# Zero rows of seven experts cut to 128 each, row ids masked by count, and one load freed of another expert's zero rows

## The chip, the cores and the metric

The kernel runs on one core of a Trainium2 chip. The metric is the device time of one execution in microseconds (us), taken as the median of several runs. The engines are PE (matrix products), PEld (its weight loads), DVE and ACT (vector and scalar work), POOL (GpSimd) and SP (which issues most DMAs). A read "chain" below is a row of steps in which each waits for the one before.

## The reference

Attention with a window of 128 positions and a distance bias runs over 8 batches, 8 heads and 576 positions; its output is 4608 rows (tokens) of 512 values. A layer of eight experts follows, in which each token goes to one expert:

```
logits = xn @ en.T / tau
expert_idx = np.argmax(logits, axis=1)
...
for e in range(E):
    mask = expert_idx == e
    h = np.maximum(x[mask] @ w1[e], 0.0)
    out[mask] = gate_w[mask, None] * (h @ w2[e])
```

w1 is 512 x 1024 and w2 is 1024 x 512 for each expert. How many tokens an expert gets is known only at run time.

## The kernel before

**Two stages.** The attention stage ends near 250 us of the trace. For each tile of 128 tokens it writes the rows with a scattering DMA from POOL (line 884) into a table in device memory, `xs`. In it each expert has a segment; a row is 521 words: 512 for the token's values (as two halves in fp16, high and low), one for the token's id, eight for its logits. The attention stage also does the first 512 rows of one expert, the "head" (`PARTS`, `HEAD`), as soon as those rows are there. The stage of the experts, `moe`, follows.

**Ranks and slots.** The experts are ranked by their counts. Rank 0 is the head's expert; what is left of it are rows 512 to 671. `SLOTS` gives each rank a fixed number of rows (672, 688, 624, 576, 544, 528, 528, 512), and `TURNS` the order of work: ranks 0, 1, 4, 3, 5, 6, 2, 7. Rows over whole blocks of 128 ("tails" of 32 or 64 rows) of several ranks share one pass through PE (`PACKED`).

**Zero rows.** A slot is larger than its expert's count, so rows past the count hold nothing. `blank(s)` (line 1318) reads the count from `n0i` or `nki` into a register of SP and writes rows from a constant `zrow` behind the last token: 704, 544, 576, 544, 544, 640 and 512 rows for ranks 1, 4, 3, 5, 6, 2 and 7, and 160 for rank 0. Each zero row has the id PAD, 2^20, which the last scatter into the output skips.

**Loads.** `rows(s)` (line 1329) then loads the slot twice: as `info` (rows on partitions, lines 1336 and 1349) and turned by the DMA as `xT` (line 1345). Rank 0 loads `info` alone (lines 1336, 1342, 1349), and PE turns it (line 1372). Both DMAs have addresses known only at run time, so the framework makes a load wait for every earlier write into `xs` that isn't declared free.

**Ids.** `row_info(s)` (line 1383) puts the ids of the slot's rows into a tile of their own: for rank 0 DVE masks those past the count `n0` with PAD (lines 1401 and 1402); for the others POOL copies them (line 1404). `put` scatters each block of 128 output rows by these ids (line 437).

**Weights and products.** The weights come in 512 KB pieces `ws` (lines 1435 and 1437, six buffers); ACT makes the high half of each (line 1455), DVE the low half (line 1453). `hidden` (line 1478) fills one of eight PSUM buffers for each of eight column groups, in one or two chunks of rows; ACT and DVE take them out as `hh` and `hl` (lines 1488 and 1486); `output` (line 1522) multiplies by w2, and DVE or ACT scale the result to `y` (lines 1536 and 1534).

**Order.** A planner written in the kernel (`Plan`) places every step as a job with an engine, an assumed length and a due time, and emits them in that order; on each engine the order is then fixed, and an engine that waits holds up all that is queued behind it. On SP, `blank` of rank 0, `blank` of rank 1 and one piece of weights stand ahead of `rows` of rank 0. After the experts' stage stands code for rows that don't fit the slots (lines 1675 to 1786); its DVE operations are placed among those of the last experts.

Of the kernel before, what the change touches and what calls it, by code (L numbers as in the profile page):

```python
# [15 lines left out]
F32 = mybir.dt.float32  # L16
I32 = mybir.dt.int32
AF = mybir.ActivationFunctionType
ALU = mybir.AluOpType
# [4 lines left out]
P = 128  # L24
# [3 lines left out]
PAD = 1 << 20  # L28
# [13 lines left out]
HEAD = PARTS[-1][1]  # L42
# [121 lines left out]
def kernel(  # L164
# [11 lines left out]
    nc = tc.nc  # L176
    NTOK, DM = out.shape
# [12 lines left out]
    def sync_dep(after, before):  # L190
        tc.add_manual_dep(
            after.ins,
            before.ins.name,
            mybir.DependencyInfo(mybir.DependencyClass.Sync, mybir.DependencyReason.DATA),
            reason="rows written by scattering DMAs",
        )
# [119 lines left out]
    def kt_(nm, shape, dt=F32):  # L316
        if nm not in sel_:
            sel_[nm] = keep.tile(shape, dt, name=nm)
        return sel_[nm]
# [37 lines left out]
    def count_ops(z):  # L357
        V = nc.vector

        def ke(nm):  # L360
            return kt_(nm, [P, E])

        return [
            ("DVE", 90, lambda: V.tensor_copy(ke("cnt"), z["cnt"])),
            ("DVE", 90, lambda: V.tensor_tensor(ke("hn"), ke("ho"), ke("cnt"), op=ALU.mult)),
            ("DVE", 90, lambda: V.tensor_reduce(kt_("n0", [P, 1]), ke("hn"), axis=AX.X, op=ALU.add)),
            ("DVE", 90, lambda: V.tensor_copy(kt_("n0i", [P, 1], I32), kt_("n0", [P, 1]))),
        ]

    def rank_ops(z):  # L370
# [919 lines left out]
    def moe(mctx):  # L1290
# [18 lines left out]
        def choose(s):  # L1309
# [5 lines left out]
            if s == 0:  # L1315
                state[s].update(w1=(w["w1h"], w["w1l"]), w2=(w["w2h"], w["w2l"]))

        def blank(s):
            e, (nb, hb), b0 = state[s]["e"], blocks(s), first_row(s) // P
            n = nc.sync.value_load(sel_["n0i"][0:1, 0:1] if s == 0 else sel_["nki"][0:1, s : s + 1], min_val=0, max_val=NTOK)  # L1320
            m = (nb - b0) * P + hb
            d = nc.sync.dma_start(
                xs[ds(e, 1), ds(n, m), :].rearrange("o (a p) c -> p (o a) c", p=32),
                zrow[0:32].unsqueeze(1).to_broadcast([32, m // 32, ROW]),
            )
            for p_ in scatters + loads:
                tc.declare_no_dep(d.ins, p_.ins, reason="rows beyond the expert's tokens, not read yet")

        def rows(s):
            cap, r0, (nb, hb) = SLOTS[s], first_row(s), blocks(s)  # L1330
            b0 = r0 // P
            e = state[s]["e"]
            xx = xt.tile([P, 2 * KT, MAXCAP], F16, tag="xT", name=f"xT_{s}")
            info = yp.tile([P, MB, ROW], F32, tag="info", name=f"info_{s}", bufs=INFOS)
            dl = [
                nc.sync.dma_start(
                    info[:, b0:nb, :],
                    xs[ds(e, 1), r0 : nb * P, :].rearrange("o (a p) c -> p (o a) c", p=P),
                )
            ]  # L1340
            if s == 0:
                dl.append(nc.sync.dma_start(info[:hb, nb, 0:DM], xs[ds(e, 1), nb * P : nb * P + hb, 0:DM].rearrange("o p c -> (o p) c")))
            else:
                x_ = xs[ds(e, 1), r0:cap, 0:DM].rearrange("o s c -> (o s) c").bitcast(F16)
                dl.insert(0, nc.sync.dma_start(xx[:, :, r0:cap], x_, transpose=True))
            if hb:
                nc.gpsimd.memset(info[:, nb, DM + 1 : ROW], 0.0)
                dl.append(
                    nc.sync.dma_start(
                        info[tail_rows(s), nb, :],  # L1350
                        xs[ds(e, 1), nb * P : nb * P + hb, :].rearrange("o p c -> (o p) c"),
                    )
                )
            loads.extend(dl)
            for d in dl:
                for p_ in scatters:
                    sync_dep(d, p_)
            state[s].update(xT=xx, info=info)

        turned = {}  # L1360
# [22 lines left out]
        def row_info(s):  # L1383
            (nb, hb), b0, info = blocks(s), first_row(s) // P, state[s]["info"]
            ids = yp.tile([P, MB], I32, tag="ids", name=f"ids_{s}", bufs=2)
            gs = yp.tile([P, MB], F32, tag="gs", name=f"gs_{s}", bufs=2)
            jobs = [(slice(0, P), slice(b0, nb), ids[:, b0:nb])]
            if hb:
                pr, pk = tail_rows(s), packs.setdefault(PACKED[s][0], {})
                if not pk:  # L1390
                    pk["ids"] = yp.tile([P, 1], I32, tag="ids2", name=f"ids2_{s}", bufs=2)
                    pk["gs"] = yp.tile([P, 1], F32, tag="gs2", name=f"gs2_{s}", bufs=2)
                jobs.append((pr, slice(nb, nb + 1), pk["ids"][pr]))
            past = yp.tile([P, MB], I32, tag="past", name=f"past_{s}", bufs=2)
            place = yp.tile([P, MB], F32, tag="place", name=f"place_{s}", bufs=1) if s == 0 else None
            for pr, bl, i_ in jobs:
                if s == 0:
                    nc.gpsimd.iota(
                        place[pr, bl], pattern=[[P, bl.stop - bl.start]], base=bl.start * P, channel_multiplier=1, allow_small_or_imprecise_dtypes=True
                    )  # L1400
                    nc.vector.tensor_scalar(past[pr, bl], place[pr, bl], sel_["n0"][pr], float(PAD), op0=ALU.is_ge, op1=ALU.mult)
                    nc.vector.tensor_tensor(i_, info[pr, bl, DM].bitcast(I32), past[pr, bl], op=ALU.max)
                else:
                    nc.gpsimd.tensor_copy(i_, info[pr, bl, DM].bitcast(I32))  # L1404
            n = nb + (hb > 0)
            n2 = yp.tile([P, MB], F32, tag="n2", name=f"n2_{s}", bufs=2)
            if hb:
                nc.gpsimd.memset(n2[:, nb : nb + 1], 1.0)  # L1408
            t = yp.tile([P, MB * (3 + E)], F32, tag="gt", name=f"gt_{s}", bufs=2)
            state[s].update(ids=ids, gs=gs, n2=n2, gate=gate_ops(n2[:, b0:n], info[:, b0:n, DM + 1 : ROW], gs[:, b0:n], t, yp.tile([P, MB], F32, tag="ry", name=f"ry_{s}", bufs=2)))  # L1410

        def span(s, a):
            return tail_rows(s) if a == blocks(s)[0] else slice(0, P)
# [124 lines left out]
        def put(s, a):  # L1538
            put_rows(packs[s]["ids"] if a == "t" else state[s]["ids"][:, a : a + 1], ys[s, a])
# [8 lines left out]
        def before(name):  # L1548
            return [(name, ORDER)]
# [15 lines left out]
        for p, s in enumerate(TURNS):  # L1565
# [12 lines left out]
                f"info{s}", "POOL", 900, lambda s=s: row_info(s), after=[f"rows{s}"], makes=[("rows", ("rows", s))],  # L1578
                uses=[("info", s)], due=t0 - 6000,
            )  # L1580
            prev = []
            for a in range(b0, nb + (hb > 0)):
                J(f"sum{s}_{a}", "POOL", 1120, lambda a=(s, a): info_sum(*a), after=[f"info{s}"], makes=[("xsum", ("xsum", s, a))], uses=[("info", s)], due=t0 - 5000)
# [56 lines left out]
            for a in todo + list(range(b0, nb)):  # L1640
                n = f"{s}_{a}"
                n_out += 1
                two = (s, a) == last_out
                key = ("y", n)
                for i in range(1 + two):
                    c = slice(i * DM // 2, (i + 1) * DM // 2) if two else slice(0, DM)
                    if a == "t":
                        mem = [m for m in PACKED if PACKED[m][0] == s]
                        PEJ(
                            f"out{n}_{i}", 24 * (216 + 22 * (len(mem) - 1)), lambda s=s: output_pack(s),  # L1650
                            [f"tail{m}" for m in mem] + w2,
                            makes=[("pt", ("ps2", n, i))], uses=[("w", 2, m) for m in mem] + [("h", s)], due=t0,
                        )
                    else:
                        PEJ(
                            f"out{n}_{i}", 24 * 216 / (1 + two), lambda x=(s, a, c): output(*x), halves + w2,
                            makes=[("pt", ("ps2", n, i))], uses=[("w", 2, s), ("h", s)], due=t0,
                        )
                    e = ("ACT", "DVE")[(n_out + i) % 2]
                    J(  # L1660
                        f"y{n}_{i}", e, 658 / (1 + two), lambda x=(s, a, e, c): scaled(*x), after=[f"out{n}_{i}"] + [f"gated{m}" for m in (mem if a == "t" else [s])],
                        makes=[] if i else [("y", key)], uses=[("ps2", n, i), key, ("rows", s)], due=t0,
                    )
                J(
                    f"put{n}", "POOL", 1150, lambda x=(s, a): put(*x), after=[f"y{n}_{i}" for i in range(1 + two)], uses=[key, ("rows", s)],
                    due=t0, dma=750,
                )
        plan.run(handed["free"])
# [155 lines left out]
```

## Time and profile before

| what | us |
|---|---|
| median of 3 runs (633.00 to 635.02) | 634.11 |
| the profiled execution | 637.05 |
| its span in the trace | 635.00 |
| PE busy | 581.0 (91%) |
| DVE, ACT, POOL busy | 360.8, 337.2, 302.0 |

The profiled execution took 2.05 us more than its span and 2.94 us more than the median. Times of the trace count from the span's start. A busy PE is not PE at its peak: how fast it runs depends on its granted clock too, of which 1.00 is 2.4 GHz and 0.50 is 1.2 GHz.

### The profile page before, as it was taken

The page shows a single profiled execution, that of the slowest core. Times are in us where ns is not written, and L with a number is a line of the kernel's source. Part 1 is how long each engine was busy: PE and PEld are TensorE (multiplying, and loading weights), DVE is VectorE, ACT ScalarE, POOL GpSimd, SP SyncE. Part 2 cuts the span into 40 slices and gives each one's busy share as a digit, 9 for nine tenths or more (in the row PEclk, how much of TensorE's full clock was granted, in tenths as well). Part 3 has the DMA queues.
Part 4 walks back from the last instruction along what each step waited for, and adds up shares of the span by engine and source line. Part 5 has one row for each costly group of instructions (what it writes and reads, how often), then busy time and mean ns, then how long its engine had stood idle before and what let it go on. Part 6 is the DMA issues. An engine that isn't in the chain of part 4 may idle for free. (4 is left out here: it accounts for less than half of the span.)

```text
span 635.0 us, 16631 instructions
## 1 busy us (share of the span) xinstructions
PE 581.0 (91%) x6273; PEld 381.7 (60%) x6273; DVE 360.8 (57%) x1381; ACT 337.2 (53%) x786; POOL 302.0 (48%) x447
## 2 busy tenths in 40 slices
PE   6899999798868999699699999899999999999993
PEld 3677677566647767276435855655856845744442
DVE  6889999889858746167191361445451454831220
ACT  4899999799758943057271550453541634410310
POOL 7689899999848896212322310234311311511111
PEclk9989999999969999989989999999999999999998
DMA  7689998999797465899999249919693077001000
GB/s 239 182 202 247 247 225 222 264 275 248 195 312 177 103 160 180 216 264 362 244 290 270 92 117 255 338 61 305 208 257 141 1 198 245 35 33 47 0 34 34
DMA packets 119954, 119.44 MB, mean 188 GB/s; under 512 B 79125, under 2 KB 80149, under 8 KB 119872
## 3 DMA queue, kind: packets, MB, share of 16 engines
q1 hardware_dynamic: 114032, 99.32, 60.5%
q0 software_dynamic: 5840, 19.05, 8.2%
q8 instruction: 50, 0.82, 0.5%
q14 instruction: 32, 0.26, 0.1%
HBM read 71.82 MB, written 28.11 MB: 157 GB/s over the span
## 5 line engine op out<-in xcount | busy, mean ns | idle before, releaser
L1478 PE MATMUL ps<-xT,w1h 128*128 128x272 f16 (+8 forms) x896 | 170.0, 291 | 3.0 <-DVE y L1536 1.9
L1478 PE MATMUL ps<-xT,w1l 128*128 128x272 f16 (+8 forms) x448 | 129.9, 291 | 0.0
L1478 PEld LDWEIGHTS <-w1h 128*128 128x128 f16 x896 | 87.6, 99 | 31.9 <-issue 3.4
L641 ACT ACTIVATE pe<-sb,nm 128x128 f32<-128x128 f32 x288 | 94.8, 393 | 16.8 <-DVE nm L633 15.3
L1522 PE MATMUL ps<-w2h,hh 128*128 128x512 f16 (+1 forms) x256 | 96.1, 375 | 6.1 <-DVE hl L1486 6.1
L437 POOL DMA_INDIRECT out_dram<-y,ids x31 | 35.8, 1155 | 137.3 <-DVE y L1536 68.4
L1522 PE MATMUL ps<-w2l,hh 128*128 128x512 f16 (+1 forms) x256 | 95.9, 375 | 0.0
L1522 PE MATMUL ps<-w2h,hl 128*128 128x512 f16 (+1 forms) x256 | 95.8, 374 | 0.0
L1486 DVE SCALAR_TENSOR_TENSOR hl<-ps,hh 128x272 f16<-128x272 f32 (+8 forms) x112 | 49.9, 463 | 70.8 <-ACT hh L1488 70.3
L1522 PEld LDWEIGHTS <-hh 128*128 128x128 f16 x512 | 50.1, 98 | 63.5 <-issue 7.9
L1488 ACT ACTIVATE hh<-ps 128x272 f16<-128x272 f32 (+8 forms) x112 | 43.7, 413 | 56.0 <-PE ps L1478 55.3
L555 ACT ACTIVATE pq<-ptp 128x512 f16<-128x512 f32 x87 | 63.9, 743 | 11.4 <-PE ptp L650 6.9
L1453 DVE SCALAR_TENSOR_TENSOR w2l<-ws,w2h 128x1024 f16<-128x1024 f32 x28 | 34.1, 1228 | 56.1 <-ACT w2h L1455 56.0
L606 PE MATMUL sc<-k,q 64*64 64x192 f32 (+1 forms) x1152 | 62.3, 333 | 0.0
L650 PE MATMUL ptp<-ident,pe 128*128 128x128 f32 x288 | 54.9, 296 | 5.7 <-ACT pe L641 4.4
L428 POOL TENSOR_TENSOR xsum<-info 128x512 f32<-128x512 f16 (+2 forms) x37 | 42.8, 1178 | 34.5 <-ACT junk L431 30.3
L1455 ACT ACTIVATE w2h<-ws 128x1024 f16<-128x1024 f32 x28 | 29.1, 1052 | 52.5 <-DMA ws<-moe_w_dram 52.5
L633 DVE CUSTOM_DVE_ANT_0 sb<-sc,tab_full 128x128 f32<-128x128 f32 x224 | 55.3, 280 | 0.2
L1478 PEld LDWEIGHTS <-w1l 128*128 128x128 f16 x448 | 44.1, 99 | 14.0 <-issue 0.4
L558 DVE SCALAR_TENSOR_TENSOR pq<-ptp,pq 128x512 f16<-128x512 f32 x57 | 42.4, 744 | 8.8 <-ACT pq L555 8.0
L650 PEld LDWEIGHTS ptp<-ident,pe 128*128 128x128 f32 x288 | 33.8, 144 | 19.1 <-ACT pe L641 12.4
L1534 ACT ACTIVATE y<-ps,gs 128x512 f32<-128x512 f32 (+1 forms) x16 | 10.7, 671 | 64.4 <-PE ps L1522 59.8
(256 smaller groups left out, 1189.6 us busy)
## 6 DMA issues: line engine op xcount, KB each, us to landing
ws<-moe_w_dram SPq DMA_DIRECT2D x56, 512.0 KB, 6.7
q<-q_dram SPq DMA_DIRECT2D x36, 256.0 KB, 4.8
ldv<-v_dram SPq DMA_DIRECT2D x36, 256.0 KB, 4.7
k<-k_dram SPq DMA_DIRECT2D x32, 256.0 KB, 4.6
info<-xs SPq DMA_DIRECT2D x5, 1042.0 KB, 6.3
stg<-moe_w_dram SPq DMA_DIRECT2D x16, 256.0 KB, 5.5
xs<-zrow SPq DMA_DIRECT2D x3, 1107.1 KB, 7.8
info<-xs SPq DMA_DIRECT2D x2, 1302.5 KB, 10.4
```

Source lines behind the costliest of these rows:

```text
L428: nc.gpsimd.tensor_tensor(o_, x[:, 0:DM], x[:, DM : 2 * DM], op=ALU.add)
L437: ins = nc.gpsimd.indirect_dma_start(out[:, :], bass.IndirectOffsetOnAxis(ap=ids, axis=0), y, None, bounds_check=NTOK - 1, oob_is_err=False)
L555: nc.scalar.activation(hi, ps, AF.Copy, scale=scale)
L558: nc.vector.scalar_tensor_tensor(lo, ps, scale, hi, op0=ALU.mult, op1=ALU.subtract)
L606: nc.tensor.matmul(sc[T, hf, j][l * REM : (l + 1) * REM, i, c0 : c0 + (n1 - n0) * REM].rearrange("p (n c) -> p n c", c=REM), qT[T][rows, h ...
L633: nc.vector.tensor_tensor_reduce(sb_t[T, hf][:, 2 * j + i, :], sc[T, hf, j][:, i, c0 : c0 + P], tab, -QS, BIG, ALU.add, ALU.min, nm_t[T, h ...
L641: nc.scalar.activation(pr_t[T, hf][:, n, :], sb_t[T, hf][:, n, :], AF.Exp, bias=nm_t[T, hf][:, n : n + 1], scale=-1.0)
L650: nc.tensor.matmul(pt.rearrange("p (l j) c -> p l j c", j=2)[:, :, j, i * REM : (i + 1) * REM], pe[:, n, :], ident.rearrange("p (l c) -> p ...
L1478: nc.tensor.matmul(ps[:, :w], a[:, kt, fs], xx[:, b + kt, c0 : c0 + w], start=(n == 0), stop=(n == len(jobs) - 1))
L1486: nc.vector.scalar_tensor_tensor(hl[:, ft, c0 : c0 + w], ps[:, :w], 0.0, hi, op0=ALU.max, op1=ALU.subtract)
L1488: nc.scalar.activation(hi, ps[:, :w], AF.Relu)
L1522: nc.tensor.matmul(ps, x[:, ft, a * P : (a + 1) * P], w[:, ft, c], start=(n == 0), stop=(n == len(jobs) - 1))
```

## The change

- `count_ops`: the integer count of rank 0, `n0i`, is at least HEAD (512).
- `blank`: for every rank but 0 the zero rows are 128 from the count on, and no longer the whole slot's length. Rank 0 keeps 160.
- `rows`: the loads of a rank are declared free of the zero rows of other ranks.
- `row_info` and the new `row_ids`: POOL no longer copies ids. For every rank POOL writes a table of places (`iota`), and DVE masks the ids by the rank's count. This is a job of its own, placed behind the sixth `hl` of the rank's first chunk; `put` waits for it.

```
-            ("DVE", 90, lambda: V.tensor_copy(kt_("n0i", [P, 1], I32), kt_("n0", [P, 1]))),
+            ("DVE", 90, lambda: V.tensor_scalar(kt_("n0i", [P, 1], I32), kt_("n0", [P, 1]), float(HEAD), None, op0=ALU.max)),
...
+        zeros = []
...
         def blank(s):
...
-            m = (nb - b0) * P + hb
+            m = (nb - b0) * P + hb if s == 0 else P
...
+            zeros.append((s, d))
...
             for d in dl:
                 for p_ in scatters:
                     sync_dep(d, p_)
+                for s_, p_ in zeros:
+                    if s_ != s:
+                        tc.declare_no_dep(d.ins, p_.ins, reason="rows of another expert")
...
-            place = yp.tile([P, MB], F32, tag="place", name=f"place_{s}", bufs=1) if s == 0 else None
+            place = yp.tile([P, MB], F32, tag="place", name=f"place_{s}", bufs=2)
             for pr, bl, i_ in jobs:
-                if s == 0:
-                    nc.gpsimd.iota(
...
-                    nc.vector.tensor_scalar(past[pr, bl], place[pr, bl], sel_["n0"][pr], float(PAD), op0=ALU.is_ge, op1=ALU.mult)
-                    nc.vector.tensor_tensor(i_, info[pr, bl, DM].bitcast(I32), past[pr, bl], op=ALU.max)
-                else:
-                    nc.gpsimd.tensor_copy(i_, info[pr, bl, DM].bitcast(I32))
+                nc.gpsimd.iota(
...
+            state[s]["known"] = jobs, past, place
...
+        def row_ids(s):
+            jobs, past, place = state[s]["known"]
+            n = sel_["n0"] if s == 0 else sel_["nk"][:, s : s + 1]
+            for pr, bl, i_ in jobs:
+                nc.vector.tensor_scalar(past[pr, bl], place[pr, bl], n[pr], float(PAD), op0=ALU.is_ge, op1=ALU.mult)
+                nc.vector.tensor_tensor(i_, state[s]["info"][pr, bl, DM].bitcast(I32), past[pr, bl], op=ALU.max)
...
+            J(
+                f"ids{s}", "DVE", 400, lambda s=s: row_ids(s), after=[f"info{s}"] + before(f"hlo{s}_{chunks(s)[0][0]}_5"),
+                uses=[("info", s), ("rows", s)], due=t0,
+            )
...
-                    f"put{n}", "POOL", 1150, lambda x=(s, a): put(*x), after=[f"y{n}_{i}" for i in range(1 + two)], uses=[key, ("rows", s)],
+                    f"put{n}", "POOL", 1150, lambda x=(s, a): put(*x), after=[f"y{n}_{i}" for i in range(1 + two)] + [f"ids{m}" for m in (mem if a == "t" else [s])], uses=[key, ("rows", s)],
```

The order of instructions on PE, ACT and SP is the same before and after. What differs on SP are the waits. SP at the end of the attention stage, before; `xs<-zrow` is the zero rows (of rank 1 here), `ws` weights, `info` the rows of rank 0, and in brackets stand the counters that a DMA waits for (HW: DMAs of SP, eight in turn; SW: DMAs of POOL, the scatters). The zero rows of rank 0 count on HW2, those of rank 1 on HW3:

```order
L1322 DMA xs<-zrow 32x22x521 [waits DMAHW2_49]
L1435 ISA
L1435 DMA ws_1_0_6444<-moe_w_dram 128x1024
L1336 ISA
L1336 DMA info_6447<-xs 128x521 [waits DMASW4_49,DMASW3_49,DMASW5_49,DMASW2_49,DMAHW0_49,DMASW1_49,DMAHW1_49,DMASW0_49,DMAHW3_49,DVE_49,DMAHW7_49,PE_49,Activation_49]
```

The same place after:

```order
L1324 DMA xs<-zrow 32x4x521 [waits DMAHW2_49]
L1444 ISA
L1444 DMA ws_1_0_6444<-moe_w_dram 128x1024
L1339 ISA
L1339 DMA info_6447<-xs 128x521 [waits DMASW3_49,DMASW4_49,DMASW2_49,DMASW5_49,DMASW1_49,DMAHW0_49,DMASW0_49,DMAHW1_49,DVE_49,DMAHW7_49,PE_49,Activation_49]
```

The wait for HW3 is gone from the load of rank 0; it stands now at the first load of rank 1.

DVE where the hidden products of rank 2 begin, before; `w2l` is the last piece of weights of rank 7, `hl` empties a PSUM buffer, and `nk`, `eb` begin the operations for rows that don't fit:

```order
L1453 SCALAR_TENSOR_TENSOR w2l_9323<-ws_7_3_9330,w2h_9322 128x1024
L1486 SCALAR_TENSOR_TENSOR hl_9381<-ps_2_0_0_9367,hh_9380 128x320
L1486 SCALAR_TENSOR_TENSOR hl_9381<-ps_2_0_1_9389,hh_9380 128x320
L1486 SCALAR_TENSOR_TENSOR hl_9381<-ps_2_0_2_9411,hh_9380 128x320
L1486 SCALAR_TENSOR_TENSOR hl_9381<-ps_2_0_3_9426,hh_9380 128x320
L1486 SCALAR_TENSOR_TENSOR hl_9381<-ps_2_0_4_9441,hh_9380 128x320
L1486 SCALAR_TENSOR_TENSOR hl_9381<-ps_2_0_5_9456,hh_9380 128x320
L1683 COPY nk_10121<-nk 128x8
L1684 COPY eb_10122<-eb 128x8
```

And after:

```order
L1696 COPY nk_10152<-nk 128x8
L1697 COPY eb_10153<-eb 128x8
L1698 COPY eb_10153<-eb 128x1
L1699 TENSOR_SCALAR nk_10152<-nk 128x1
L1709 TENSOR_SCALAR it_10167<-it 128x46
L1717 TENSOR_TENSOR low<-iota_10161 128x81
L1700 TENSOR_TENSOR late<-nk_10152,np 128x1
L1701 TENSOR_TENSOR nk_10152<-nk_10152,late 128x1
L1705 TENSOR_TENSOR ovr<-nk_10152,capt 128x9
L1711 TENSOR_TENSOR big<-ovr,it_10167 128x414
L1715 TENSOR_REDUCE nb<-big 128x9
L1495 SCALAR_TENSOR_TENSOR hl_9409<-ps_2_0_0_9393,hh_9408 128x320
```

Eleven operations for rows that don't fit now stand between the last `w2l` and the first `hl`, and the rest of them between the next five `hl`. On POOL the tables that they read (`capt`, `it`) stand one output scatter earlier than before.

## Rows read from the trace of the kernel before

**Rows 1.** What PE waited for, 255 to 630 us: us in total, times, longest
```profile
PE turn L1372 <- DMA info<-xs: 6.3, 1, 6.3
PE ps L1522 <- DVE hl L1486: 6.1, 1, 6.1
PE ps L1478 <- DVE y L1536: 1.9, 1, 1.9
PE ps L1478 <- DVE hl L1486: 0.7, 1, 0.7
```

**Rows 2.** Busy time by stretch: us, PE, PEld, DVE, ACT, POOL, PEclk, DMA share, GB/s
```profile
269.20:274.00 4.80, 4.38 (x39) 3.99 (x40) 3.57 (x8) 3.27 (x5) 2.13 (x2) 0.50 0.92 317
274.00:312.70 38.70, 38.64 (x292) 26.25 (x291) 20.38 (x41) 19.34 (x41) 9.36 (x15) 1.00 1.09 282
318.70:322.00 3.30, 3.23 (x9) 1.18 (x9) 2.41 (x6) 2.05 (x6) 1.73 (x2) 0.53 0.98 366
406.80:412.80 6.00, 5.95 (x49) 4.76 (x49) 2.54 (x7) 1.50 (x5) 0.97 (x1) 1.00 0.99 252
421.00:624.00 203.00, 203.00 (x1293) 119.23 (x1292) 85.51 (x188) 71.50 (x152) 49.26 (x66) 1.00 0.41 122
```

**Rows 3.** Timeline at the first wait: start us, us, engine, line, what
```profile
250.34 0.96 POOL L884 DMA_INDIRECT xs<-rows_buf,di  x1 [0.19 <-issue]
...
255.66 0.39 SPq L1435 DMA_DIRECT2D ws<-moe_w_dram  x1
...
265.31 0.37 SPq L1336 DMA_DIRECT2D info<-xs  x1
...
262.91 0.69 ACT L1012 ACTIVATE y_head<-ps_head,gs_head 128x512 f32<-128x512 f32 x1 [6.75 <-PE ps_head L1005]
...
269.20 0.37 PE L1372 MATMUL turn<-ident,info 128*128 128x128 f16 x2 [6.32 <-DMA info<-xs]
```

**Rows 4.** DMA issues: what, count, KB each, median us from issue to landing
```profile
xs<-zrow SPq DMA_DIRECT2D x1, 1432.8 KB, 10.0
...
xs<-rows_buf,di POOLq DMA_INDIRECT x36, 4.8
...
xs<-zrow SPq DMA_DIRECT2D x1, 325.6 KB, 3.8
```

**Rows 5.** Timeline of the chain that ends the second wait
```profile
293.11 0.37 SPq L1322 DMA_DIRECT2D xs<-zrow  x1
...
301.20 0.39 SPq L1336 DMA_DIRECT2D info<-xs  x1
...
311.30 1.06 SPq L1437 DMA_DIRECT2D ws<-moe_w_dram  x1
...
315.99 1.06 ACT L1455 ACTIVATE w2h<-ws 128x1024 f16<-128x1024 f32 x1 [11.34 <-DMA ws<-moe_w_dram]
...
318.77 0.59 PE L1522 MATMUL ps<-w2h,hh 128*128 128x512 f16 x1 [6.06 <-DVE hl L1486]
```

**Rows 6.** Timeline of what precedes the third and fourth wait
```profile
372.45 0.37 SPq L1322 DMA_DIRECT2D xs<-zrow  x1
379.90 0.40 SPq L1336 DMA_DIRECT2D info<-xs  x1
...
416.03 0.43 POOL L1404 COPY ids<-info 128x4 int32<-128x4 int32 x2 [7.99 <-issue]
```

**Rows 7.** The first of the id operations of DVE
```profile
271.11 0.20 DVE L1401 TENSOR_SCALAR past<-place,n 128x1 int32<-128x1 f32 x1
```

**Rows 8.** Timeline of DVE and PE in the hidden products of rank 2
```profile
538.94 2.08 DVE L1486 SCALAR_TENSOR_TENSOR hl<-ps,hh 128x320 f16<-128x320 f32 x5
...
542.52 0.16 DVE L1683 COPY nk<-nk 128x8 f32<-128x8 f32 x1
...
548.52 0.58 DVE L1702 TENSOR_REDUCE nb<-big 128x9 f32<-128x414 f32 x1
...
544.70 0.42 PE L1478 MATMUL ps<-xT,w1h 128*128 128x304 f16 x2
```

More of the change, by code (lines that the diff above doesn't have):

```diff
@@ L1394, in row_info @@
             past = yp.tile([P, MB], I32, tag="past", name=f"past_{s}", bufs=2)
-            place = yp.tile([P, MB], F32, tag="place", name=f"place_{s}", bufs=1) if s == 0 else None
+            place = yp.tile([P, MB], F32, tag="place", name=f"place_{s}", bufs=2)
             for pr, bl, i_ in jobs:
-                if s == 0:
-                    nc.gpsimd.iota(
-                        place[pr, bl], pattern=[[P, bl.stop - bl.start]], base=bl.start * P, channel_multiplier=1, allow_small_or_imprecise_dtypes=True
-                    )
-                    nc.vector.tensor_scalar(past[pr, bl], place[pr, bl], sel_["n0"][pr], float(PAD), op0=ALU.is_ge, op1=ALU.mult)
-                    nc.vector.tensor_tensor(i_, info[pr, bl, DM].bitcast(I32), past[pr, bl], op=ALU.max)
-                else:
-                    nc.gpsimd.tensor_copy(i_, info[pr, bl, DM].bitcast(I32))
+                nc.gpsimd.iota(
+                    place[pr, bl], pattern=[[P, bl.stop - bl.start]], base=bl.start * P, channel_multiplier=1, allow_small_or_imprecise_dtypes=True
+                )
+            state[s]["known"] = jobs, past, place
             n = nb + (hb > 0)
@@ L1580, in moe @@
             )
+            J(
+                f"ids{s}", "DVE", 400, lambda s=s: row_ids(s), after=[f"info{s}"] + before(f"hlo{s}_{chunks(s)[0][0]}_5"),
+                uses=[("info", s), ("rows", s)], due=t0,
+            )
             prev = []
```

## The prediction

> **What bounds the kernel now.** PE was busy 581 of 635 us, so I first asked the trace where PE waits in the stage of the experts. From 255 us on there are four waits of more than half a microsecond [rows 1]: 6.3 us for the load of rank 0, 6.1 us at rank 1's output, then 1.9 and 0.7 us. Second came the busy times by stretch [rows 2]. Here the reader is to see three things. Behind each of the two long waits PE ran at a granted clock of 0.50 and 0.53 (1.2 GHz), for 4.8 and 3.3 us; behind the wait of 1.9 us it stood at 1.00. Between the first two waits PE is busy for 38.64 of 38.70 us, so that whole block (rank 1's hidden products) moves as one when its start moves. And from 421 to 624 us PE is busy for all of 203.00 us: whatever is won before 421 reaches the end of the kernel in full, and whatever delays PE there costs in full. The DMA engines are full (share 1.09) until 312.7 and have room after 421 (0.41).
>
> Third, I followed each wait to its cause. **First wait** [rows 3]: PE ended the head at 262.88 (269.20 less 6.32) and turned rank 0's rows at 269.20, when `info` had landed. That load was issued at 265.31, although SP had been free since 256.05 (255.66 + 0.39); it waited for the zero rows of rank 1. These are 1432.8 KB, landing 10.0 us after their issue [rows 4], and the change takes them from its list of waits. **Second wait** [rows 5]: zero rows of rank 4 issued at 293.11; its load could be issued only at 301.20, when they had landed; the turned load follows on SP; then at 311.30 the first piece of w2 for rank 4 is issued, 18.2 us after the zero rows. ACT stands 11.34 us waiting for that piece before it makes `w2h` (315.99), and the outputs of rank 1 on DVE and PE are held by what is queued on ACT behind it. PE goes on at 318.77. **Third and fourth** [rows 6]: zero rows of rank 5 took from 372.45 to 379.90, which sets back the weights behind them and so DVE's queue; and POOL's id copy at 416.03, which had to wait until an earlier `put` had read the same id tile, held up the gate computation and DVE.
>
> **The change part by part.** The sum is made against the profiled execution, 637.05 us, which lies 2.94 above the median.
>
> *Load of rank 0 freed: -5.55.* What it still waits for are its own zero rows (325.6 KB, 3.8 us, so landed near 254.4 or 255) and the scatters, the last issued at 250.34 and landing after 4.8 us, thus 255.1 [rows 3, 4]. SP issues one shortened set of zero rows and one piece of weights ahead of it, so I take 256.4, which is 8.9 us earlier. From issue to PE's turn took 3.9 us before; that gives 260.3. PE ends the head at 262.88, but the turn needs a PSUM bank that ACT empties as `y_head` until 263.60 (262.91 + 0.69). So PE starts at 263.65: 5.55 earlier. If the load took as long as the longest zero rows, 10.0 us, it would land at 266.4 and the gain would be 2.8.
>
> *Half clock behind the first wait: -1.6.* PE was busy 4.38 us at 0.50. A wait of 0.8 us is shorter than the 1.9 after which the clock stayed at 1.00 [rows 2], so I expect full clock. All of it would give 4.38 / 2 = 2.2; I take 1.6, since the first two of these microseconds also wait for ACT and DVE, which copy the turned rows. Bounds 0 and 2.2. Rank 1's hidden products then end at 312.7 - 7.15 = 305.55.
>
> *Second wait: -3.5.* The chain starts from SP, which was free 8.9 us earlier; some weight buffers on the way come free with PE (7.15 earlier), so I let rank 4's zero rows be issued 8.4 us earlier, at 284.7. They then shrink from 544 to 128 rows, 1107 to 267 KB (548 and 128 rows of 521 words; 840 KB less). In a full queue at 366 GB/s [rows 2] 840 KB are 2.3 us. The bounds are wider: from 325.6 KB at 3.8 to 1432.8 KB at 10.0 us [rows 4] is 5.6 us per MB, so 840 KB could be 4.7; and nothing, if the landing waits only on weights ahead of it. I take 2.3, since the DMA engines are full there. `w2h` moves by 8.4 + 2.3 = 10.7 and PE's resumption to 318.77 - 10.7 = 308.1. PE is there at 305.55, so 2.5 us of wait remain of 6.06.
>
> [...]
>
> *Half clock behind the second wait: -1.5.* 3.23 us at 0.53 take 1.5 us less at full clock. Whether a wait of 2.5 us brings the clock down, between the 1.9 that didn't and the 6.1 that did, is not in the rows; bounds 0 and 1.5. I take 1.5, since 2.5 is nearer to 1.9.
>
> *Third and fourth wait: -2.6.* Rank 5's zero rows alone took 7.45 us; at 267 KB they should be nearer to 3.8, so its load and the weights behind it come 3.6 us earlier, more than the 1.9 us. The id copies leave POOL, and with them the wait for a tile that a `put` still reads. Bounds 0 and 2.6. What is late next there are weights' buffers that wait for DVE; I see none within 3 us.
>
> *Ids on DVE: 0.* Two operations for each of twelve groups, 24 of about 0.2 us [rows 7], 4 us in all where DVE is idle for more than half of the time (85.51 busy of 203). They are behind the sixth `hl` and PE waits for none of them; `put` does, a chunk later. If the cover were gone they would cost up to 0.4 us a rank. The iotas on POOL replace copies of like length, and need no load: 0.
>
> *DVE's order in front of rank 2: 0, up to 2.1.* Eleven operations, 5.75 us by their durations from the first to the last [rows 8], now precede the first `hl`, which started at 538.94. It would start at 544.7 and end at 545.2; PE wants that buffer at 544.70 for the second chunk. So it is late by at most 0.5, and the other operations between the next five `hl` are about as long together: the last of the six, done at 542.6 before, could come at 554.1, where PE reaches that buffer at 544.7 + 5 x 1.5 = 552.2 (twelve matmuls of 304 columns at 2.4 GHz each). Hence 2.1 (0.5 and 1.9 overlap). The cover is that rank 7's last weights, which gate DVE there, come earlier as rank 7's zero rows shrink too. That PE doesn't wait in between is the value I take.
>
> Sum: -5.55 - 1.6 - 3.5 - 1.5 - 2.6 = -14.75, thus 622.3 traced and 619.4 as a median.
>
> **Rivals.**
> 1. *The second wait vanishes.* If the blanks save 4.7 rather than 2.3, PE waits 0.1 there: 617.0. For it: the slope between the two rows. Against: the full queue.
> 2. *Half clock after the remaining wait.* Then 1.5 come back: 620.9. The rows show the fall behind 6.3 and 6.1 us, and none behind 1.9. The Trainium skill, "TensorE: Matmul & The Clock Gate", section "HAM oscillation — how this bites in real kernels", tells that waits for DMA between blocks let each next block start at half clock; the two long waits agree, the 1.9 us wait doesn't.
> 3. *Given back at the second wait.* DMA engines are full from 269 to 322, so weights may arrive no earlier though issued earlier. Then only the removed 840 KB count: PE resumes 2.3 us earlier, and with the later 2.6 the time is 634.1 - 4.9 = 629.2. For it: share 1.09. Against: the engines carry some 2 MB less by then, and SP's chain, not the bytes, ended last.
> 4. *The change doesn't do what it says.* The load of rank 0 still waits as long on another counter that zero rows share, or a short write lands as late as a long one: 634.1. Against: the issue order shows that counter HW3 is gone there, and 325.6 KB landed in 3.8 us, 1432.8 in 10.0.
> 5. *Slower: rank 2's first `hl` behind the eleven operations.* These read tables (`capt`, `it`) that POOL makes, and PE has no idle time from 421 to 624. Every microsecond that the first `hl` comes after 544.7 is lost. It eats the whole gain once it is 14.75 us late (on the old time scale 559.5), and it is slower by over 0.3% from 561.4 on; at 563 the time would be 638. Against: POOL stands before that point with these tables early, one `put` ahead of the old place.
>
> **How the numbers follow.** 0.3% is 1.9 us, about what a measurement of this kernel can tell from no change. The forecast, 619.4, has 0.60; rival 1 (617.0) 0.11; rival 2 (620.9) 0.09; rival 3 (629.2) 0.11; rival 4 (634.1) 0.06; rival 5 (638) 0.03. Faster is all but the last two, 0.91. The range: at the low end rival 1 with the last half microsecond, 616.5. At the high end the low bounds together: the chain moves by 8.4 alone, the clock falls, the third and fourth wait stay and DVE costs 2.1, which is -8.4 + 2.1 = -6.3 or 627.8; with not all of them at once, 627. It leaves out rivals 3 to 5, 0.20.
>
> **What would show it.** In the changed kernel's trace: the load of rank 0 issued near 256.4 and PE's turn near 263.65, released by ACT and not by a load; clock 1.00 from there to 305; one wait of about 2.5 us near 305, still behind ACT's `w2h`; zero rows landing within 6 us each; no wait near 405 and 419 (now some 12 us earlier); no wait of PE on `hl` where rank 2's second chunk starts. The forecast is wrong if PE waits as long near 305 as before, if the turn is still released by a load, or if PE is idle after 420.

## The result, and the profile after

The changed kernel takes 625.0 us (median of 4 runs, 623.96 to 627.27) against 633.8 before: a ratio of 0.987, with an interval of 0.983 to 0.990. It is faster, as forecast, but by 8.8 us where 14.7 were forecast. Measured once more, next to new runs of the kernel before, it was 0.982 (0.973 to 0.991). Medians here are of all runs, while the ratios leave out the slow ones (over 1.5% above the fastest run of the same kernel), so the two need not agree exactly.

| what, us | before | after |
|---|---|---|
| median | 633.8 | 625.0 |
| profiled execution's span | 635.0 | 622.1 |
| end of the head on PE | 262.9 | 259.8 |
| from there to the span's end | 372.1 | 362.3 |

One thing has to be known before the spans are compared. The attention stage ends at a different time in each execution: over the thirteen traces of this case PE ended the head between 257.1 and 268.4 us, in kernels whose code up to there is the same but for the count `n0i` and the first zero rows. So all times below are counted from the end of the head, which is the start of PE's turn less the idle time in front of it. Counted so, the change is worth 9.8 us in these two traces.

What PE waited for after the change, from 245 to 620 us (us in total, times, longest), all that is over a quarter of a microsecond:

```profile
PE ps L1531 <- DVE hl L1495: 5.9, 1, 5.9
PE turn L1378 <- ACT y_head L1012: 0.8, 1, 0.8
PE ps L1487 <- ACT xT L1385: 0.4, 1, 0.4
```

The four waits of [rows 1] are all gone. The turn is released by `y_head` after 0.8 us and not by a load. But there is a new wait of 5.9 us. Its line (1531) is again an output, but of rank 0 this time: an earlier place than that of the old second wait. Busy time by stretch (us, PE, PEld, DVE, ACT, POOL, PEclk, DMA share, GB/s): rank 0's hidden products, then what follows the new wait, then rank 1's hidden products, its first outputs, and the long stretch behind 412 us:

```profile
261.90:268.90 7.00, 6.88 (x96) 6.61 (x95) 4.75 (x5) 3.71 (x4) 4.11 (x5) 1.00 1.17 274
274.90:279.30 4.40, 4.40 (x11) 1.57 (x11) 4.27 (x12) 2.33 (x9) 2.93 (x2) 0.50 1.03 394
282.30:310.30 28.00, 28.00 (x194) 18.79 (x193) 20.94 (x38) 17.95 (x38) 9.73 (x14) 1.00 0.92 285
310.30:313.60 3.30, 3.30 (x17) 1.53 (x16) 3.20 (x11) 2.07 (x6) 0.18 (x1) 1.00 0.81 224
412.00:612.00 200.00, 199.82 (x1279) 117.90 (x1277) 83.54 (x179) 67.33 (x140) 45.67 (x63) 1.00 0.34 107
```

The half clock that stood behind the first wait [rows 2] is gone from there and stands behind the new wait: 0.50 for 4.4 us, which is 2.2 us lost. Rank 1's outputs begin without a wait and at full clock.

The new wait's chain, read backwards in the timeline (start, us, engine, line, what, idle before and what ended it):

```profile
255.71 1.00 POOL L437 DMA_INDIRECT out_dram<-y_head,ids_head  x1 [2.92 <-DVE y_head L1014]
...
257.95 1.15 POOL L428 TENSOR_TENSOR xsum<-info 128x512 f32<-128x512 f16 x1 [0.64 <-DMA info<-xs]
262.89 2.16 POOL L428 TENSOR_TENSOR xsum<-info 32x512 f32<-32x512 f16 x1 [3.79 <-DMA out_dram<-y_head,ids_head]
265.33 1.69 POOL L437 DMA_INDIRECT out_dram<-y_head,ids_head  x1 [0.28 <-POOL xsum L428]
...
259.86 0.69 ACT L1012 ACTIVATE y_head<-ps_head,gs_head 128x512 f32<-128x512 f32 x1 [6.74 <-PE ps_head L1005]
...
274.13 1.28 ACT L1497 ACTIVATE hh<-ps 128x160 f16<-128x160 f32 x6 [8.52 <-DMA out_dram<-y_head,ids_head]
...
274.90 0.58 PE L1531 MATMUL ps<-w2h,hh 128*128 128x512 f16 x1 [5.93 <-DVE hl L1495]
```

PE waits for `hl`, `hl` for `hh`, and `hh` on ACT has been idle for 8.52 us behind a scatter of `y_head`, the head's last one. ACT made that `y_head` at 259.86 to 260.55, but POOL issued its scatter at 265.33, since POOL had two sums (`xsum`) ahead of it, and the second of these waited 3.79 us for the scatter before. It landed 8.4 us later, at 273.7. The first `hh` carries the waits for all memory that its stage takes over from the attention stage, those for the scatters of `y_head` among them, so it may start only when the last scatter has landed. In the kernel before POOL and ACT did the same steps in another order:

```profile
263.87 0.98 POOL L437 DMA_INDIRECT out_dram<-y_head,ids_head  x1 [3.99 <-ACT y_head L1012]
...
269.03 2.38 POOL L428 TENSOR_TENSOR xsum<-info 128x512 f32<-128x512 f16 x2 [3.61 <-DMA info<-xs]
...
275.87 1.26 ACT L1488 ACTIVATE hh<-ps 128x160 f16<-128x160 f32 x5
```

There the scatter went out 0.3 us behind `y_head`, ahead of the sums, landed 3.8 us later, near 267.7, and `hh` started at 275.87 without a wait. That the change turned this order round can be read from the instructions of POOL, before (left out: small operations) and after:

```
L437 DMA out_dram<-y_head_1_6375,ids_head_6035 4608x512 [waits DMASW7_49,Activation_49]
L428 TENSOR_TENSOR xsum_4_6531<-info_6447 128x512 [waits DMAHW5_49]
L428 TENSOR_TENSOR xsum_5_6561<-info_6447 32x512 [waits DMASW7_49,DMAHW7_49,DMASW6_49,Pool_49]

L428 TENSOR_TENSOR xsum_4_6527<-info_6447 128x512 [waits DMAHW5_49]
L428 TENSOR_TENSOR xsum_5_6557<-info_6447 32x512 [waits DMASW7_49,DMAHW7_49,DMASW6_49,Pool_49]
L437 DMA out_dram<-y_head_1_6375,ids_head_6035 4608x512 [waits Activation_49,Pool_49]
```

No line of the diff names this scatter, and the section on the change, which lists what moved on POOL, doesn't have it. It belongs to the attention stage and the sums to the stage of the experts; how the two stages are interleaved on an engine is decided when the program is built, and there the short zero rows let the sums go first. In the programs of the experiments below, wait_kept has the new order and ids_only the old one, and these two differ in the length of the zero rows alone: it is the length that turns the order round.

### The profile page after: what moved, and what is told of

It reads as the page before. It is cut to its first block, busy times and chain, and to the rows that moved or that the text cites. A ratio compares the mean times of both kernels' runs of the same rounds, so it can differ in the third digit from the quotient of the medians.

```text
span 622.1 us, 16660 instructions
## 1 busy us (share of the span) xinstructions
PE 576.6 (93%) x6273; PEld 380.1 (61%) x6273; DVE 375.0 (60%) x1405; ACT 339.6 (55%) x786; POOL 303.4 (49%) x447
## 4 chain that ended last, share of the span: by engine, by line
PE 65%; POOL 10%; DMA 9%; DVE 8%; issue 3%; ACT 3%; SPq 0%; POOLq 0%; ACTq 0%; DVEq 0%
PE ps L1487 26%; PE ps L1531 26%; DMA xT<-rows_buf 4%; PE ps_head L958 3%; PE av L738 3%; DMA out_dram<-y_head,ids_head 2%; DVE sb L633 2%; POOL mp L688 2%; PE ptp L650 2%; PE ps_t L1521 2%; DVE pq L558 2%; DMA stg<-moe_w_dram 2%; PE sc L606 2%; POOL md L688 1%; POOL xs L884 1%
## 5 line engine op out<-in xcount | busy, mean ns | idle before, releaser
L437 POOL DMA_INDIRECT out_dram<-y,ids x31 | 33.3, 1075 | 141.7 <-DVE y L1545 70.1
L1497 ACT ACTIVATE hh<-ps 128x272 f16<-128x272 f32 (+8 forms) x112 | 45.0, 416 | 83.7 <-PE ps L1487 70.4
L428 POOL TENSOR_TENSOR xsum<-info 128x512 f32<-128x512 f16 (+2 forms) x37 | 44.5, 1223 | 63.7 <-ACT junk L431 58.7
L650 PE MATMUL ptp<-ident,pe 128*128 128x128 f32 x288 | 53.5, 293 | 5.9 <-ACT pe L641 3.4
L1543 ACT ACTIVATE y<-ps,gs 128x512 f32<-128x512 f32 (+1 forms) x16 | 10.7, 671 | 73.5 <-PE ps L1531 68.9
L1545 DVE TENSOR_SCALAR y<-ps,gs 128x512 f32<-128x512 f32 (+1 forms) x16 | 11.7, 732 | 61.6 <-PE ps L1531 61.6
```

The costliest lines, as they stand in the source:

```text
L428: nc.gpsimd.tensor_tensor(o_, x[:, 0:DM], x[:, DM : 2 * DM], op=ALU.add)
L650: nc.tensor.matmul(pt.rearrange("p (l j) c -> p l j c", j=2)[:, :, j, i * REM : (i + 1) * REM], pe[:, n, :], ident.rearrange("p (l c) -> p ...
L1497: nc.scalar.activation(hi, ps[:, :w], AF.Relu)
```

## The experiments

Times from the end of the head to the end of the span, next to the ratio to the kernel before in the same set of runs (medians in us). The last column is of one trace each, and two traces of the same kernel differ there by 0.6 to 5.9 us:

| kernel | median, of before | ratio (95%) | from head's end |
|---|---|---|---|
| changed kernel | 625.0, 633.8 | 0.987 (0.983 to 0.990) | 362.3 |
| after2 (the same) | 627.9, 636.3 | 0.982 (0.973 to 0.991) | 361.0 |
| put_first | 616.7, 634.0 | 0.972 (0.967 to 0.977) | 355.4 |
| put_first2 (the same) | 620.6, 638.5 | 0.974 (0.967 to 0.981) | 356.0 |
| wait_kept | 620.7, 634.0 | 0.978 (0.972 to 0.984) | 356.9 |
| wait_kept2 (the same) | 627.0, 638.5 | 0.978 (0.969 to 0.987) | 362.8 |
| first_wait | 624.9, 636.3 | 0.980 (0.975 to 0.986) | 360.0 |
| first_wait2 (the same) | 621.4, 638.5 | 0.978 (0.972 to 0.984) | 357.4 |
| free_only | 633.0, 634.0 | 0.997 (0.992 to 1.003) | 370.9 |
| ids_only | 635.2, 634.0 | 1.001 (0.995 to 1.007) | 369.9 |
| first_long4 | 624.0, 636.3 | 0.977 (0.971 to 0.983) | 360.4 |
| first_long1 | 628.1, 636.3 | 0.987 (0.983 to 0.992) | 362.4 |

### The scatter back in its place: put_first

```
-            row_sum(x[pr], state[s]["info"][pr, a, :])
+            d = row_sum(x[pr], state[s]["info"][pr, a, :])
+            if s == 0:
+                tc.add_manual_dep(
+                    d.ins,
+                    out_sc[HEAD // P - 1].ins.name,
+                    mybir.DependencyInfo(mybir.DependencyClass.NoSync, mybir.DependencyReason.DATA),
+                    reason="behind the head's last scatter",
+                )
```

(`row_sum` returns its instruction for this.) On POOL the scatter then stands ahead of the two sums, and nothing else moves on any engine.

> The changed kernel, with one edge added: POOL's sums over rank 0's rows stand behind the head's last output scatter, as in the kernel before, and no longer ahead of it. Theory (the moved scatter): in the changed kernel this scatter was issued at 265.33 us and landed at 273.72, and ACT's first hh of rank 0 started at 274.13, after it; PE then waited 5.9 us at rank 0's output and ran at half clock for some 4 us. With the scatter issued right behind y_head, near 260.6 us, it lands 7 to 8 us later (as the one before it did: 7.1), near 268, PE's wait at rank 0's output falls to 0 to 1.5 us and the half clock is gone. PE then is at rank 1's output some 7 us earlier than its weights, so a wait of about 3 us comes up there, behind ACT's w2h: 625.0 - 4.4 = 620.6 us. Rival (the queue): the scatter lands behind the turned load of rank 1 whenever it is issued, near 272 to 274: 624 to 625 us. Rival (another release): hh waits for another of the transfers in its list: 625.0 us and the same wait of 5.9 us.

Measured: 616.7 us, 17.3 below the kernel before. The waits of PE:

```profile
PE ps L1538 <- DVE hl L1502: 1.2, 1, 1.2
PE turn L1378 <- ACT y_head L1012: 0.8, 1, 0.8
PE ps L1494 <- ACT xT L1385: 0.4, 1, 0.4
```

And the timeline of POOL and ACT:

```profile
258.12 1.00 POOL L437 DMA_INDIRECT out_dram<-y_head,ids_head  x1 [3.51 <-ACT y_head L1012]
259.14 1.18 POOL L428 TENSOR_TENSOR xsum<-info 128x512 f32<-128x512 f16 x1
266.52 1.15 POOL L428 TENSOR_TENSOR xsum<-info 32x512 f32<-32x512 f16 x1 [6.20 <-DMA out_dram<-y_head,ids_head]
...
266.71 1.28 ACT L1504 ACTIVATE hh<-ps 128x160 f16<-128x160 f32 x6 [3.80 <-DMA out_dram<-y_head,ids_head]
```

The same edge from scatter to `hh` is still there (3.80 us of ACT, 8.6 us from issue to `hh`), but it now begins 4.5 us earlier, counted from the head's end, and of PE's wait 1.2 us are left. The second sum now waits 6.20 us, which delays nothing that PE needs. The clock behind the short wait stayed full:

```profile
267.50:272.80 5.30, 5.30 (x25) 2.43 (x25) 4.89 (x17) 2.72 (x11) 3.45 (x7) 1.00 1.04 263
```

So the moved scatter is shown to be what the changed kernel lost: the queue alone didn't hold it. The expected time, 620.6, was 3.9 us too high, in the main because the wait of 3 us at rank 1's output did not come up (here 0; 1.7 us in put_first2). The second measurement bears out the first: 0.974, and 356.0 us from the head's end.

### Only the declaration: free_only

The kernel before, with this alone (`zeros` collects the zero rows as in the change):

```
+                for s_, p_ in zeros:
+                    if s_ != s:
+                        tc.declare_no_dep(d.ins, p_.ins, reason="rows of another expert")
```

> The kernel before with the declaration alone: the loads of a rank don't wait for zero rows of other ranks, which keep their full length; ids as before. On POOL the scatter stands ahead of the sums, as before. Theory: rank 0's load is issued near 256.4 us, behind 1433 KB of zero rows in the DMA queues; the weights issued at 255.66 landed there at 266.3, so the load lands near 266.5 and PE's first wait falls from 6.3 to about 3.6 us; the SP chain moves as far. About 2.7 us at the first and as much at the second wait, which is the same gain, not twice: 633.8 - 2.7 = 631 us. Rival (what the prediction took): the load lands 3.9 us after its issue, PE's first wait is 0.8 us: 627 us or less.

Measured: 633.0 against 634.0 us, a ratio of 0.997: no difference that can be told from none. Timeline of the load and of PE's turn:

```profile
253.68 1.72 SPq L1339 DMA_DIRECT2D info<-xs  x1
...
264.76 0.48 PE L1378 MATMUL turn<-ident,info 128*128 128x128 f16 x3 [4.85 <-DMA info<-xs]
```

The load is issued 6.2 us before PE ends the head, and yet PE gets it 11.1 us after the issue, where 3.9 us lay between the two before [rows 3]. The rows of 1433 KB that it no longer waits for were issued ahead of it by the same SP. What was a wait on a counter became a late landing; that it comes from these rows is shown below by first_long1, which has the rows of rank 1 alone at the old length. PE's waits in this kernel:

```profile
PE ps L1528 <- DVE hl L1492: 5.5, 1, 5.5
PE turn L1378 <- DMA info<-xs: 4.9, 1, 4.9
PE ps L1484 <- DVE hl L1492: 1.7, 1, 1.7
PE ps L1484 <- DVE y L1542: 1.6, 1, 1.6
```

### Only the ids: ids_only

The changed kernel without the declaration, and with zero rows of the old length:

```
-            m = (nb - b0) * P + hb if s == 0 else P
+            m = (nb - b0) * P + hb
...
-                for s_, p_ in zeros:
-                    if s_ != s:
-                        tc.declare_no_dep(d.ins, p_.ins, reason="rows of another expert")
```

> The changed kernel with zero rows of full length and without the declaration: what is left of the change are the ids on DVE, the iotas on POOL in place of copies, and DVE's order in front of rank 2. Theory: 24 short operations of DVE lie beside idle time, and the wait of 0.7 us behind POOL's id copy goes: 633.8 - 0.7 = 633.1 us, PE's waits of 6.3, 6.1 and 1.9 us as in the kernel before. Rival (the order costs): PE waits for hl where rank 2's second chunk starts, up to 2.1 us: 635 to 636 us.

Measured: 635.2 against 634.0 us, a ratio of 1.001: neither cost nor gain is clear of noise. The wait behind POOL's id copy (0.7 us in [rows 1]) is gone, the one behind `y` is not:

```profile
PE turn L1375 <- DMA info<-xs: 6.3, 1, 6.3
PE ps L1528 <- DVE hl L1492: 4.1, 1, 4.1
PE ps L1484 <- DVE y L1542: 1.9, 2, 1.7
```

One thing that the expectation names is not in this kernel: with long zero rows DVE has the old order in front of rank 2. The first `hl` there, of 320 columns, run ahead of the operations for rows that don't fit, which begin with `nk`:

```profile
538.72 1.68 DVE L1492 SCALAR_TENSOR_TENSOR hl<-ps,hh 128x320 f16<-128x320 f32 x4
...
543.53 0.16 DVE L1693 COPY nk<-nk 128x8 f32<-128x8 f32 x1
```

So this run prices the ids and the iotas, and not that order.

### Without the declaration: wait_kept and first_wait

wait_kept is the changed kernel without the three lines of the declaration (the second half of the diff above); first_wait is put_first without them. Each was measured twice.

> The changed kernel without its declaration: the load of rank 0 waits for the zero rows of rank 1 again, which are 128 rows here. On POOL the head's last scatter stands behind the sums over rank 0's rows, as in the changed kernel. Theory: 261 KB land some 3.5 us after their issue, before PE ends the head, so the wait costs PE nothing at the first place: the load is issued near 257.5 to 259, the turn is still released by y_head, and the time is that of the changed kernel, 625.0 us within 1. Then the declaration is worth nothing beside the cut. Rival (the chain counts): SP is 3 to 4 us later with all that follows, the wait at rank 1's output comes up again with 3 us: 628 us.

> wait_kept once more (no declaration, scatter behind the sums). Theory: with the wait, less of rank 1's load is in the queues when the scatter of y_head 1_0 goes out, so the sums, and with them the last scatter, come earlier than in the changed kernel; PE waits 2 to 3 us at rank 0's output and nowhere else for over 1 us: 357 us from the head's end, 0.978. Rival: the wait is as long as in the changed kernel, 5 to 6 us, and the first time was luck: 0.982 to 0.986.

wait_kept was faster than expected at first: PE's wait at rank 0's output was 2.8 us. In the second trace it was 6.1 us, as in the changed kernel (5.9, and 5.1 in after2). The two lines, of wait_kept and of wait_kept2:

```profile
PE ps L1528 <- DVE hl L1492: 2.8, 1, 2.8
```

```profile
PE ps L1528 <- DVE hl L1492: 6.1, 1, 6.1
```

With the scatter behind the sums the length of this wait differs from run to run: POOL's second sum waited 1.06 us for the scatter before it in wait_kept and 4.31 us in wait_kept2, and so the last scatter was issued 2.2 and 4.4 us behind the head's end (5.5 in the changed kernel). By the wait the rival of the second expectation is right, and the short wait was luck; by the ratio it is not, since 0.978 came both times, where the changed kernel had 0.987 and 0.982. The intervals overlap. So no gain of the declaration is shown in the changed kernel, and whether it costs something there stays open.

> The changed kernel with the scatter put back ahead of POOL's sums (as in put_first) and without the declaration, so that the load of rank 0 waits for rank 1's 128 zero rows again. Theory (the length counts, the declaration doesn't): the zero rows land some 3.2 us after their issue, the load is issued some 3 us later than in put_first and still lands before y_head ends; PE's turn is released by y_head, and the scatter meets less of rank 1's load in the queue. The time is that of put_first, 616.7 us, within 1.5. Rival (the SP chain counts): all that follows on SP is 3 us later, w2h of rank 4 comes too late for rank 1's output, PE waits about 2.5 us there: 619.5 us or more.

> first_wait once more (no declaration, scatter ahead of the sums). Theory: no wait at rank 0's output, but 2 to 3 us at rank 1's, with half clock behind it, as the first time: 360 us from the head's end, 0.980. Rival: that wait was of one execution: 357 us or less, 0.975.

With the scatter ahead of the sums the traces lie to one side: from the head's end 360.0 and 357.4 us without the declaration, 355.4 and 356.0 with it. PE's waits over half a microsecond in first_wait, then the busy times behind the first of them:

```profile
PE ps L1535 <- DVE hl L1499: 2.5, 2, 2.4
PE turn L1375 <- ACT y_head L1012: 0.8, 1, 0.8
PE ps L1491 <- DVE y L1549: 0.6, 1, 0.6
PE ps L1491 <- DMA xT<-xs: 0.5, 1, 0.5
```

```profile
309.50:313.50 4.00, 4.00 (x11) 1.47 (x11) 3.05 (x7) 2.68 (x8) 1.62 (x2) 0.57 0.65 213
```

The load of rank 0 is in time all the same (the turn is released by `y_head`), so its own wait is free; what is late are rank 1's turned load and the weights for rank 1's output, which SP issues later. In the second traces the wait at rank 1's output is the same without the declaration (first_wait2) and with it (put_first2):

```profile
PE ps L1535 <- DVE hl L1499: 1.7, 1, 1.7
```

```profile
PE ps L1538 <- DVE hl L1502: 1.7, 1, 1.7
```

Behind both the clock was full; first_wait2 has besides a wait of 1.1 us for the turned load. So the rival of first_wait2 is right for that trace (357.4 us; expected were 360). The ratios of first_wait (0.980, 0.978) and put_first (0.972, 0.974) have intervals that overlap in both pairs, and in the second pair, run side by side, the medians are 621.4 and 620.6. The traces say 1.4 to 4.6 us for the declaration; 2.6 us lie between the two traces of first_wait alone. So a gain of the declaration is not clear of noise.

### The old length for one rank: first_long4 and first_long1

put_first with this line, for rank 4, and the same with `(0, 1)` for rank 1:

```
-            m = (nb - b0) * P + hb if s == 0 else P
+            m = (nb - b0) * P + hb if s in (0, 4) else P
```

> put_first with the zero rows of rank 4 alone at their old length, 544 rows. It prices the step of the prediction at the second wait. In put_first the zero rows of rank 4 landed 6.4 us after their issue and w2h ran at 297.67 us, with PE at rank 1's output from 300.7 without a wait. Theory (the prediction's step): 840 KB more in a full queue take 2.3 us, w2h comes 2.3 us later and PE waits about 2 us there: 616.7 + 2 = 618.7 us. Rival 1 (slope of the two rows of zero rows): 4.7 us later, a wait of about 4.3 us and perhaps half clock behind it: 621 to 622.5 us. Rival 2 (it was the freed SP alone): no wait, 616.7 us.

The profiled execution of first_long4 was long ahead of the head's end (268.35 us), so only what follows is read. From issue of rank 4's zero rows to the issue of its load:

```profile
290.39 0.38 SPq L1324 DMA_DIRECT2D xs<-zrow  x1
...
299.96 0.39 SPq L1339 DMA_DIRECT2D info<-xs  x1
```

That is 9.6 us, and 6.5 in put_first:

```profile
278.74 0.37 SPq L1324 DMA_DIRECT2D xs<-zrow  x1
...
285.25 0.39 SPq L1339 DMA_DIRECT2D info<-xs  x1
```

so 840 KB cost 3.1 us there (3.2 against put_first2). PE waits 4.9 us at rank 1's output, with half clock behind it (0.55):

```profile
PE ps L1538 <- DVE hl L1502: 4.9, 1, 4.9
```

```profile
315.60:318.60 3.00, 3.00 (x8) 1.05 (x8) 2.22 (x3) 1.93 (x4) 1.60 (x2) 0.55 1.00 382
```

In all 4.4 to 5.0 us from the head's end (360.4 against 356.0 and 355.4). Rival 1 is nearest: in the trace the length of this one rank's zero rows brings back most of the second wait, 4.9 of 6.1 us. By the ratios it costs less: 0.977 against 0.972 and 0.974, with intervals that overlap.

> put_first with the zero rows of rank 1 alone at their old length, 704 rows, declared free as in the changed kernel. Theory (the queue): rank 0's load, issued right behind them, waits in the DMA queues as in free_only, where PE's first wait was 4.9 us and the half clock behind it cost some 1.6 us: 616.7 + 4.1 + 1.6 = 622.4 us. Rival (the wait on the semaphore was the cause): the load lands in time, 616.7 us.

```profile
PE turn L1378 <- DMA info<-xs: 6.4, 1, 6.4
```

Although declared free, the load comes as late as in the kernel before (6.3 us of wait), and the half clock comes back with it:

```profile
270.50:274.50 4.00, 4.00 (x31) 4.00 (x31) 3.61 (x3) 3.55 (x6) 1.02 (x4) 0.50 1.03 401
```

It takes 362.4 us from the head's end, 6.4 to 7.0 more than put_first. So the first wait needs the cut more than the declaration: with short zero rows it is gone with or without the declaration (first_wait), with long ones it stays with or without it (first_long1, free_only).

## Why the prediction was right or wrong

The time lies in the range and the sign is right; the forecast of 619.4 was 5.6 us too low. That the miss was no larger is in part luck: the whole gain of the first two steps was lost, and the second wait gave more than was asked of it. None of the signs that were to show the forecast wrong came up, and none of them looked at what follows the turn. By its steps:

- **First wait and half clock behind it (-5.55, -1.6): right there, and lost at once.** The load was issued in time, the turn was released by `y_head` after 0.78 us, and the clock was 1.00 from there on. But 5.9 us of wait and 2.2 us of half clock came up 8 us later. Rank 1's hidden products began 22.5 us after the head's end (282.3 less 259.8) against 21.5 before: of 7.15 us nothing was left.
- **The step that failed** is that POOL's part was priced at 0. The prediction weighed the iotas against the copies ("replace copies of like length, and need no load") and looked at the tables for rank 2; it did not go through what else had changed place on POOL. The last scatter of the head had moved behind two sums, of which one waits for a transfer, and `hh` waits for that scatter. At the third and fourth wait the prediction asked what is late next; at the first it did not: behind the turn stands `hh`, and what it waits for was not looked up. put_first shows the step's price: 5.0 to 6.9 us from the head's end.
- **Second wait (-3.5, 2.5 to remain): the chain was right, its sum too small.** In the changed kernel no wait remained, in part because PE came late itself. With the scatter in its place 0 and 1.7 us remained. From the head's end ACT made the `w2h` that ends this chain at 53.1 us before, at 40.6 in put_first and 41.4 in put_first2: 12.5 and 11.7 us earlier, where 10.7 were taken. The zero rows were issued 8.6 and 7.8 us earlier (8.4 were taken), and from there to the load it was 1.6 and 1.7 us less (2.3 were taken; against long rows in the same place, in first_long4, 3.1). The term that was missing lies behind the load: SP was busy for 8.7 us with the turned load before, and for 7.0 in both. The rival in which the second wait vanishes has the time of put_first (616.7 against its 617.0) by luck: no step shows its 4.7 us for the zero rows.
- **Half clock behind it (-1.5): right in the changed kernel,** since there was no wait. The rival of half clock after a short wait did occur, in one of the two traces of first_wait.
- **Third and fourth wait (-2.6): right.** Neither is there. ids_only splits them: without the id copies the 0.7 us is gone, while the 1.7 us at `y` stays until the zero rows are short.
- **Ids on DVE, and DVE's order in front of rank 2 (0 each): right.** For the ids ids_only measured 1.001. The order is in the changed kernel and not in ids_only; there PE was busy for 199.82 of 200 us behind 412, so the rival that ended slower had no part.
- **What was attributed to the declaration** ("load of rank 0 freed") is mostly the cut's. The prediction let the load land 3.9 us after its issue whatever stood ahead of it in the queue; free_only shows 11.1 us behind long zero rows. In the changed kernel the cut removes both, so the number held.

In sum, from the head's end: +1.0 at rank 1's start (-7.15 + 5.9 + 2.2), -6.1 for the second wait, -1.5 and -2.6 as forecast, which is -9.2 of the -9.8 seen.

## What to carry to other kernels

When a change shortens a transfer, go through the whole new order of every engine and not only the instructions that the diff names: the order may have changed round a neighbour, and a wait that is won at one instruction can be lost at the next one whose list of waits was covered before. Taking a dependency away from a load helped here only where the data issued ahead of it was short too; cutting the data came first, and what the declaration adds to it, 1.4 to 4.6 us in the traces, is not clear of noise. The better kernel of this study is put_first, at 0.972 and 0.974 of the kernel before: the change with one edge that keeps the head's last scatter ahead of the sums.

## What the runs showed of the hardware

- The granted clock fell behind a wait of 2.4 us (0.57 over the next 4 us, first_wait) but not behind one of 2.8 us in wait_kept:

```profile
277.10:282.40 5.30, 5.30 (x25) 2.43 (x25) 4.89 (x17) 2.72 (x11) 3.01 (x3) 1.00 1.07 239
```

  Of the others behind the head, waits of 4.9 us and more were all followed by 0.50 to 0.59, the 4.1 us of ids_only by 0.77 and then 0.50 (2 us each), and the waits of 1.7 us in put_first2 and first_wait2 by 1.00. So between 2 and 3 us the length of the wait alone doesn't tell whether the clock falls; what else does was not settled.
- The same scatter of the head's last rows took 3.8, 8.2 and 8.4 us from issue to landing: in the kernel before (issued at 263.87), in put_first (258.12) and after the change (265.33):

```profile
out_dram<-y_head,ids_head POOLq DMA_INDIRECT x1, 3.8
```

```profile
out_dram<-y_head,ids_head POOLq DMA_INDIRECT x1, 8.2
```

```profile
out_dram<-y_head,ids_head POOLq DMA_INDIRECT x1, 8.4
```

  In the first case SP issued rank 1's load only at 269.19, when the scatter had landed; in the other two that load of 1302 KB and the turned one behind it had been issued before the scatter (from 254.75 and from 257.62). That they are what the scatter met in the DMA engines fits these times; no run tests it.
